# A kernel of recurrence and feed-forward network with its order written out: another list of steps and of PSUM tiles, the same operations

## The chip, the cores and the metric

One core of one Trainium2 chip runs the whole program. The metric is the device time of one execution in microseconds.

## The reference

Two blocks, one behind the other. The first is a recurrence over 768 tokens for 4 sequences of 8 heads, with a state of 40 by 40 per head:

```python
for t in range(S):
    y[:, :, t] = einsum('bhd,bhde->bhe', r_t, state)
    Sa = einsum('bhde,bhe->bhd', state, a_t)
    state = state * w_t[:, :, None, :] - einsum('bhd,bhe->bhde', Sa, b_t)
    state = state + einsum('bhd,bhe->bhde', v_t, k_t)
```

Its output, turned to 3072 tokens of 320 numbers, goes through an RMS norm with a gain and a gated feed-forward network with 1536 inner channels:

```python
xn = x / sqrt(mean(x * x) + 1e-6) * rms_g
g = xn @ w_gate
out = (g * sigmoid(g) * (xn @ w_val)) @ w_out
```

The three weight matrices arrive as 64-bit numbers and are narrowed to 32 bits on the chip; all else is 32 bits wide.

## The kernel before, in words

The work is cut into parts, each a function that notes steps. A step is one instruction on VectorE (DVE), ScalarE (ACT) or GpSimd (POOL), one DMA issue on SP, POOL or ACT, or one group of matmuls on TensorE (PE).

- `narrow` (12 slices of the weights, two parts each): load a part of the 64-bit weights, take the words apart on ScalarE and VectorE, and write the 32-bit slice to `sW` in DRAM.
- `front(c)` for each of 24 chunks of 32 tokens: load the tokens, turn them on TensorE, and build by doubling (levels of 2, 4, 8, 16 tokens, the group `gramk`) the decayed keys `KN` and the triangular matrix `LT`, which `where` steps copy from PSUM.
- `inverse(c)` (`early_inverse(c)` for the first four chunks): invert the triangular matrix by short VectorE steps (`tmp`, `Yi` or `M`), with `LT` and the inverse carried through DRAM (`sB`, `sY`).
- `main(c)`: the chunk itself: `state`, `lower`, `update`, `score`, the five `level` products, `y0`, and at the end the norm and the turned activations `xg`.
- `feed(g)` for each pair of chunks: 12 slices of the feed-forward network, two at a time: `h64` (8 passes through TensorE) and `h` (8 passes) for gate and value, SiLU on ScalarE (`sg`), the product on VectorE (`hT`), `out` (4 passes) summed up in `po`. After the first two groups six slices are kept in the buffers `wf` and the others come again from `sW`.

All 5924 steps, with what each needs, are noted first; nothing is issued then. `Plan.issue` goes through the text `ORDER` from front to back and issues one step a word; a `-` issues a pair of idle matmuls. Each word counts from the first step that has not been issued yet:

```python
i = first + int(word)
gone.add(i)
while first in gone:
    first += 1
```

So `ORDER` fixes the order on each engine and on each DMA queue, and engines run their queues strictly in order. What waits for what on the chip follows from the data alone.

A part of the steps works in PSUM. There are three pairs of banks (`ps0` to `ps2`) besides `po`, and 499 uses of a pair ("rooms"), from the first matmul that writes to the last reader. The text `PAIRS` has one digit a room that says which pair it takes; a room's first matmul waits until the room before it in the same pair has been read. The helpers record each operation at one line: L485 VectorE, L508 ScalarE copies, L511 ScalarE scalings, L524 DMAs, L527 matmuls, L530 turns.

Of the kernel before, what the change touches and what calls it, by code (L numbers as in the profile page):

```python
# [58 lines left out]
525 0 0 673 547 535 676 0 539 6 541 545 - 15 542 813 531 812 532 16 0 500 822 16 542 543 820 664 6 546 819 8 7 547  # L59
749 810 672 548 684 706 681 549 682 750 550 666 501 638 504 551 752 9 502 552 - 809 0 655 543 495 544 0 544 13 668  # L60
810 545 22 676 662 6 546 30 7 547 21 665 - 674 549 8 550 548 0 666 657 672 483 544 663 1139 660 32 658 671 23 675
807 5 0 662 0 802 801 538 662 804 667 803 673 805 817 666 15 809 7 808 672 539 8 17 822 1054 724 663 671 1064 670
834 846 600 1 479 540 806 480 541 9 481 10 0 0 673 804 8 539 15 672 9 671 813 666 812 540 541 479 852 674 0 15 722
806 541 17 22 807 725 0 667 714 807 717 722 799 715 483 - 800 808 484 805 806 818 820 819 724 814 801 725 829 810
# [4 lines left out]
737 738 1028 742 740 739 743 744 745 0 0 744 745 8 531 690 533 532 534 842 535 694 1042 14 695 - 1024 832 837 838  # L69
839 836 1045 1044 1043 1059 1047 1034 1064 1035 1046 536 1051 1052 1063 1074 1027 696 697 1037 1062 15 16 537 17  # L70
1036 1050 18 19 1075 1048 1073 913 1049 - 914 916 840 841 1058 843 917 919 921 918 920 844 538 539 845 846 540 542
# [6 lines left out]
622 396 705 480 624 699 706 703 942 702 700 337 338 339 340 543 541 701 - 548 341 342 343 344 704 345 346 349 348  # L78
347 - 350 549 397 941 546 398 708 952 - 709 720 354 715 698 634 635 714 399 400 716 721 733 729 718 353 717 636 719
# [1012 lines left out]
```

## Time and profile before

| | |
|---|---|
| median of 3 runs | 1012.74 us (1011.0 to 1017.76) |
| profiled execution | 1018.17 us |
| its span, from the first to the last instruction | 1016.1 us |
| mean granted TensorE clock | 0.972 |
| busy: TensorE, VectorE, ScalarE, GpSimd | 934.5, 794.0, 507.6, 310.7 us |
| moved by DMA | 112.97 MB |

Busy times are unions of an engine's instructions; PEld is the loading of weights into TensorE, which overlaps its matmuls. A wait is put down to what released it; "issue" stands for a wait that nothing in the program is seen to end. Times in a timeline row are the start from the span's beginning and the length, in us; a number in brackets is the engine's idle time just before, with its releaser.

### The profile page before, as it was taken

What the parts mean: (1) busy time and instruction counts of PE and PEld (TensorE: products, weight loads), DVE (VectorE), ACT (ScalarE), POOL (GpSimd) and SP (SyncE); (2) the same over time, 40 slices, a digit from 0 to 9 for tenths busy, and PEclk for the clock granted to TensorE, in tenths of its full rate; (3) what the DMA queues carried; (4) which work ended last, traced back from release to release, by engine and by line L of the source; (5) the groups of instructions that cost most, each with busy time, mean ns of one, the idle gap of its engine ahead of it and who ended that gap; (6) DMA issues with size and microseconds to landing.
All of it is one profiled execution on the core that took longest, in us unless ns stands there. A gap on an engine that the chain in (4) does not pass through costs nothing.

```text
span 1016.1 us, 55137 instructions
## 1 busy us (share of the span) xinstructions
PE 934.5 (92%) x24360; PEld 761.6 (75%) x24360; DVE 794.0 (78%) x2699; ACT 507.6 (50%) x1163; POOL 310.7 (31%) x554
## 2 busy tenths in 40 slices
PE   2647789799999999999999999999999999999998
PEld 2546677678787787888887888777878888778776
DVE  7798877778888988887988787877888897886310
ACT  5767784545446445544544454455454455443311
POOL 8635232241431342340350350331431431210000
PEclk9998679989999999999999999999999999999999
DMA  9975575744543635443544433624625533523122
GB/s 182 213 176 135 149 187 123 197 91 106 131 83 88 147 73 122 107 80 79 143 90 104 109 76 77 153 47 108 143 57 129 122 64 95 125 52 96 45 72 72
DMA packets 163534, 112.97 MB, mean 111 GB/s; under 512 B 124512, under 2 KB 142880, under 8 KB 163296
## 3 DMA queue, kind: packets, MB, share of 16 engines
q1 hardware_dynamic: 144928, 86.48, 34.3%
q0 software_dynamic: 16192, 22.64, 13.1%
q8 instruction: 191, 3.13, 1.3%
q10 hardware_dynamic: 2176, 0.33, 0.3%
q14 instruction: 47, 0.39, 0.1%
HBM read 93.39 MB, written 15.99 MB: 108 GB/s over the span
## 4 chain that ended last, share of the span: by engine, by line
PE 73%; DVE 13%; DMA 7%; issue 4%; ACT 1%; SPq 1%; POOL 1%; DVEq 0%; ACTq 0%; POOLq 0%
PE ps L527 52%; PE po L527 14%; PE ps L530 6%; DVE tmp L485 2%; DVE LT L485 2%; DVE Yi L485 2%; SPq L524 1%; DMA wf<-in_moe_w_gate_dram 1%; DVE K L485 1%; DMA wf<-sW 1%; DVE y L485 1%; DVE wf L485 1%; DVE As L485 1%; DMA wf<-in_moe_w_out_dram 1%; DMA rn<-in_r_dram 1%
## 5 line engine op out<-in xcount | busy, mean ns | idle before, releaser
L527 PE MATMUL ps<-xg,wf 128*128 128x256 f32 (+1 forms) x1728 | 356.5, 396 | 1.5 <-issue 1.2
L527 PEld LDWEIGHTS ps<-xg,wf 128*128 128x128 f32 (+1 forms) x1728 | 265.0, 192 | 50.1 <-issue 12.4
L527 PE MATMUL po<-wf,hT 128*128 128x320 f32 x576 | 178.9, 445 | 0.0
L485 DVE TENSOR_TENSOR tmp<-Yi,M 128x60 f32<-128x60 f32 (+24 forms) x620 | 130.3, 210 | 16.3 <-DMA M<-sB 1.7
L485 DVE TENSOR_TENSOR Yi<-Yi,tmp 128x60 f32<-128x60 f32 (+24 forms) x620 | 130.1, 210 | 15.5
L527 PEld LDWEIGHTS po<-wf,hT 128*128 128x128 f32 x576 | 103.2, 189 | 35.4 <-issue 0.7
L505 ACT ACTIVATE sg<-ps 128x512 f32<-128x512 f32 x72 | 43.0, 597 | 154.3 <-PE ps L527 142.6
L524 POOL DMA_DIRECT2D VU<-in_v_dram x92 | 53.7, 586 | 175.7 <-PE ps L527 127.9
L485 DVE TENSOR_TENSOR hT<-ps,sg 128x512 f32<-128x512 f32 x72 | 49.5, 687 | 69.5 <-ACT sg L505 69.2
L485 DVE TENSOR_TENSOR K<-K,T 128x512 f32<-128x512 f32 (+1 forms) x192 | 93.4, 496 | 9.7 <-PE ps L530 3.9
L527 PE MATMUL ps<-Ab,K 40*60 40x56 f32 (+2 forms) x4608 | 83.5, 228 | 15.5 <-DVE K L485 4.3
L527 PEld LDWEIGHTS ps<-Ab,K 40*60 40x60 f32 (+2 forms) x4608 | 74.6, 138 | 30.7 <-issue 13.6
L524 POOL DMA_DIRECT2D kbn<-in_k_dram x92 | 53.4, 583 | 135.7 <-PE ps L527 126.2
L508 ACT COPY KN<-ps 128x640 f32<-128x640 f32 x96 | 65.8, 693 | 43.6 <-PE ps L527 19.3
L508 ACT COPY K<-K 128x256 f32<-128x256 f32 (+1 forms) x168 | 72.3, 444 | 24.0 <-DVE K L485 8.8
L527 PEld LDWEIGHTS ps<-As,KN 128*40 128x40 f32 x3072 | 68.0, 127 | 18.3 <-issue 10.5
L485 DVE TENSOR_TENSOR As<-ps,msi 128x256 f32<-128x256 f32 (+1 forms) x168 | 69.8, 454 | 15.1 <-ACT As L511 8.6
L527 PE MATMUL ps<-As,KN 128*40 128x32 f32 x3072 | 73.8, 208 | 8.3 <-issue 6.0
L524 POOL DMA_DIRECT2D kbn<-in_b_dram x92 | 53.8, 587 | 88.0 <-PE ps L527 84.4
L524 POOL DMA_DIRECT2D wn<-in_w_dram x92 | 51.8, 567 | 68.6 <-DVE KN L485 32.3
L485 DVE TENSOR_TENSOR y<-y,ps 128x256 f32<-128x256 f32 x119 | 49.9, 419 | 18.8 <-PE ps L527 15.2
L485 DVE COPY_PREDICATED LT<-near,ps 128x384 f32<-128x384 uint32 (+2 forms) x72 | 52.3, 727 | 6.3 <-PE ps L527 5.4
(134 smaller groups left out, 1427.5 us busy)
## 6 DMA issues: line engine op xcount, KB each, us to landing
wf<-sW SPq DMA_DIRECT2D x82, 480.0 KB, 4.7
M<-sB SPq DMA_DIRECT2D x80, 128.0 KB, 2.9
rn<-in_r_dram SPq DMA_DIRECT2D x24, 160.0 KB, 5.2
out_dram<-o SPq DMA_DIRECT2D x48, 80.0 KB, 2.6
kbn<-in_b_dram POOLq DMA_DIRECT2D x92, 40.0 KB, 3.3
VU<-in_v_dram POOLq DMA_DIRECT2D x92, 40.0 KB, 2.7
kbn<-in_k_dram POOLq DMA_DIRECT2D x92, 40.0 KB, 3.2
wan<-in_w_dram POOLq DMA_DIRECT2D x46, 80.0 KB, 4.2
```

Of the source, the lines that this page charges most:

```text
L485: plan.add("DVE", kind, lambda at: fn(at(o), *m(at)), [o], aps(*args))
L505: plan.add("ACT", "act", lambda at: nc.scalar.activation(at(o), at(a), f, **kw), [o] + aps(acc), [a])
L508: plan.add("ACT", "copy", lambda at: nc.scalar.copy(at(o), at(a)), [o], [a])
L524: plan.add(by, "dma", lambda at: queue.dma_start(out=o, in_=i), [o], [i])
L527: return o, lhsT, rhs, lambda at: nc.tensor.matmul(at(o), lhsT, rhs, start=start, stop=stop, skip_group_check=True)
L530: return o, i, ident, lambda at: nc.tensor.transpose(at(o), i, ident)
```

## The change

Only the two texts differ. `ORDER` has the same 5944 words (5924 steps and 20 idle pairs) in another sequence, with its first 461 words and its last two steps as they were. `PAIRS` has the same 499 digits' places, of which 292 hold another digit. No function, operation, tile or number of buffers is changed. According to its description the order was searched by small moves, with every block of an engine's instructions taken to arrive later than was measured.

The diff is some 190 lines of numbers on either side; its beginning and its other part:

```diff
 156 157 654 663 681 665 519 684 678 679 682 877 664 675 163 166 167 164 868 29 171 680 165 168 677 434 435 30 523
-524 525 436 437 568 571 572 569 181 190 46 48 570 158 685 526 527 528 529 170 581 582 676 149 573 179 28 585 180
-574 182 870 191 169 686 690 530 531 532 533 534 535 536 537 538 539 687 172 683 540 541 199 542 694 200 202 543 544
...
+524 525 436 437 568 38 46 28 180 878 158 870 190 48 181 191 170 202 526 527 201 528 529 530 686 531 169 532 533 182
+534 535 570 536 537 149 572 538 200 539 569 540 179 541 571 542 543 685 581 683 544 545 546 547 573 548 582 549 199
...
 PAIRS = """
-1020102202110121001212001202211200201011102220012212101222200002201012220212110102101210221011100120120101220001012100
+1020102202110121111222000022000201112210001210020212001022110011120001020221210212021002122211202201212001112120210
...
```

More of the change, by code (lines that the diff above doesn't have):

```diff
@@ L48 @@
 156 157 654 663 681 665 519 684 678 679 682 877 664 675 163 166 167 164 868 29 171 680 165 168 677 434 435 30 523
[10 rows of a table removed]
[L59 to L62, printed above, removed]
@@ L63 @@
-834 846 600 1 479 540 806 480 541 9 481 10 0 0 673 804 8 539 15 672 9 671 813 666 812 540 541 479 852 674 0 15 722
-806 541 17 22 807 725 0 667 714 807 717 722 799 715 483 - 800 808 484 805 806 818 820 819 724 814 801 725 829 810
[4 rows of a table removed]
-737 738 1028 742 740 739 743 744 745 0 0 744 745 8 531 690 533 532 534 842 535 694 1042 14 695 - 1024 832 837 838
-839 836 1045 1044 1043 1059 1047 1034 1064 1035 1046 536 1051 1052 1063 1074 1027 696 697 1037 1062 15 16 537 17
-1036 1050 18 19 1075 1048 1073 913 1049 - 914 916 840 841 1058 843 917 919 921 918 920 844 538 539 845 846 540 542
[6 rows of a table removed]
@@ L78 @@
-622 396 705 480 624 699 706 703 942 702 700 337 338 339 340 543 541 701 - 548 341 342 343 344 704 345 346 349 348
-347 - 350 549 397 941 546 398 708 952 - 709 720 354 715 698 634 635 714 399 400 716 721 733 729 718 353 717 636 719
[35 rows of a table removed]
-763 765 774 764 592 773 766 388 593 771 594 654 595 389 772 596 434 597 655 598 599 600 646 601 602 658 - 603 712
[24 rows of a table removed]
-364 365 561 366 558 367 423 7 574 569 8 368 0 368 369 370 371 569 411 372 567 577 570 373 374 580 375 405 - 376 578
[3 rows of a table removed]
-- 422 423 643 424 0 726 424 0 424 567 570 739 967 372 751 571 977 572 425 573 959 640 574 426 575 428 576 978 427
@@ L145 @@
-577 723 578 642 579 968 652 580 724 429 581 970 582 375 583 0 583 372 584 727 585 732 373 586 587 652 762 1126 737
-430 731 3 653 735 375 654 743 1127 734 429 - 728 1 588 589 729 730 431 739 742 749 432 435 746 741 590 591 745 592
-744 642 593 594 595 437 596 645 597 644 598 747 599 756 600 755 646 748 436 771 754 759 757 760 761 601 602 643 740
-751 438 439 767 603 604 605 752 763 655 766 433 - 656 764 606 753 775 607 608 389 773 765 609 610 659 772 390 611
[5 rows of a table removed]
-357 546 591 358 328 359 360 361 540 404 544 536 405 557 406 408 407 0 - 544 536 542 537 538 550 0 409 552 0 545 550
[10 rows of a table removed]
@@ L165 @@
-747 758 755 756 757 623 624 761 625 626 627 628 629 760 630 740 751 444 754 741 631 440 - 445 753 446 752 763 659
[23 rows of a table removed]
-362 363 192 364 402 365 366 563 367 564 368 558 413 - 369 404 370 371 574 372 415 373 573 5 555 374 406 572 408 389
[5 rows of a table removed]
-41 202 49 203 738 356 50 341 40 204 205 350 42 358 43 253 206 353 44 165 256 207 254 366 208 368 209 45 - 359 360
[9 rows of a table removed]
-- 556 364 225 365 366 412 565 226 367 368 411 409 575 414 407 573 406 0 575 416 403 368 573 369 370 371 412 372 373
[27 rows of a table removed]
[10 rows of a table added]
+673 547 535 676 0 539 6 541 545 - 15 542 813 531 812 532 16 0 500 822 16 542 543 820 6 546 664 819 8 7 547 810 672
@@ new lines @@
+548 749 684 706 681 549 682 550 666 501 638 504 551 665 502 809 9 750 0 495 542 - 742 543 544 0 544 13 668 22 810
+545 676 662 6 30 546 7 21 674 8 547 0 656 - 540 483 541 539 32 666 657 672 23 544 663 1139 660 658 0 666 670 802 0
+662 0 802 801 804 803 805 538 662 666 7 667 673 817 15 809 8 808 672 663 539 17 822 1054 724 671 1064 670 834 846
+600 1 479 540 806 480 541 9 481 10 0 0 673 804 8 539 672 15 9 671 813 666 812 540 541 479 852 674 0 15 722 806 541
+17 22 807 725 676 0 807 714 717 722 799 715 483 - 800 808 484 805 806 818 820 819 724 814 801 725 829 668 817 669
[4 rows of a table added]
@@ new lines @@
+742 740 739 743 744 745 0 0 744 745 8 531 690 533 532 534 842 535 694 1042 14 695 - 1024 832 837 838 839 836 1045
+1044 1043 1059 1047 1034 1064 1035 1046 536 1051 1052 1063 1074 1027 696 697 1037 1062 15 16 537 17 1036 1050 18 19
+1075 1048 1073 913 1049 - 914 916 840 841 1058 843 917 919 921 918 920 844 538 539 845 846 540 542 1076 847 1072
[6 rows of a table added]
+480 624 699 706 703 942 702 700 337 338 339 340 543 541 701 - 548 341 342 343 344 704 345 346 349 348 347 - 350 549
+397 941 546 398 708 952 - 709 720 354 715 698 634 635 714 399 400 716 721 733 729 718 353 717 636 719 730 637 351
[36 rows of a table added]
@@ new lines @@
+606 607 608 434 710 609 610 554 701 611 612 613 711 646 435 774 662 666 1 777 663 756 775 432 436 776 437 668 - 448
[23 rows of a table added]
+558 566 365 366 367 423 7 574 569 8 368 0 368 369 370 371 569 411 372 567 577 570 373 374 580 375 405 - 376 578 413
+377 579 419 507 0 398 404 500 416 409 716 406 0 406 411 574 412 407 575 409 573 226 416 421 572 227 369 370 229 417
+422 228 418 414 554 720 566 721 719 509 709 419 420 423 726 371 424 722 372 425 712 373 374 375 426 376 377 427 727
+970 731 3 - 730 4 710 378 651 728 381 979 729 562 5 379 508 565 711 380 428 736 579 0 574 0 574 725 0 568 574 575
@@ new lines @@
+421 576 569 0 576 421 373 422 577 423 0 577 578 970 579 423 580 581 424 639 582 725 425 583 640 374 967 427 584 428
+585 375 977 426 586 723 734 642 587 968 652 739 724 727 429 959 588 1127 589 738 0 977 727 - 746 732 589 1 590 750
+731 653 375 372 728 429 654 762 3 771 652 748 734 1127 735 744 743 430 736 729 747 749 591 745 592 730 742 739 431
+432 435 741 556 755 756 760 754 759 642 593 594 437 595 646 596 761 597 598 645 599 757 600 740 643 601 436 602 644
+751 438 439 767 752 763 603 655 604 605 766 433 - 656 606 764 753 607 775 608 389 609 765 773 610 647 611 774 390
[5 rows of a table added]
@@ new lines @@
+357 358 359 535 545 404 540 536 543 406 546 405 547 544 408 0 - 556 406 536 537 538 0 409 358 359 315 557 546 0 409
[11 rows of a table added]
+389 668 775 441 390 773 772 660 765 632 667 670 666 768 451 - 673 662 672 665 767 778 556 770 762 453 771 661 769
[22 rows of a table added]
+389 402 192 364 365 564 366 413 - 367 404 572 368 563 369 554 575 403 370 5 371 415 574 372 555 373 573 558 374 406
[11 rows of a table added]
+351 531 352 189 538 532 0 - 527 539 726 345 544 736 556 346 12 528 229 727 11 531 201 529 347 728 4 348 349 532 725
+202 542 324 735 350 555 401 351 543 352 6 353 405 354 537 403 402 552 355 404 356 0 356 537 398 324 357 358 552 532
@@ L233 @@
+359 540 539 360 4 549 533 534 547 535 544 553 6 548 563 7 407 561 565 361 550 362 0 - 558 355 400 552 356 551 537
[29 rows of a table added]
 """
 PAIRS = """
-1020102202110121001212002211200201011102220012212101222200002201012220212110102101210221011100120120101220001012100
-0102202021021021110211202211221001122102012222002200002010212222110112021012020112110021010021101100100210001102220
-2222120001100121202121222012220211100100221101011011202011210112221221112100100100010202210011011021222022221002020
-0020100220112100111020021122212220211212110101012000002221112010012120201112122211102102111002010100000201101010101
@@ L240 @@
-211221011020020202020112210001002212121
+1020102202110121111222000022000201112210001210020212001022110011120001020221210212021002122211202201212001112120210
+1210010102122101101202210022001110112012012222002111101011220200012021000110201210120121120022121122100211001120000
+0221210021120222202021202102221111100211220010102000221101211112002120112000100122100212211000101120212022221000120
+0121100220021221011010211022202211011211112102022101002220220120012100201221201110102101022101010000201022022002022
@@ L241 @@
+212102210212010210010220102112111210210
 """
```

314 rows, old and new, of the table ORDER are left out of this document.

## The prediction

> **What bounds the kernel now.** I read the page first, then the table of stages, TensorE's waits in the long stage, and the timeline around single waits.
>
> ```profile
> span 1016.1 us, 55137 instructions
> PE 934.5 (92%) x24360; PEld 761.6 (75%) x24360; DVE 794.0 (78%) x2699; ACT 507.6 (50%) x1163; POOL 310.7 (31%) x554
> q8 instruction: 191, 3.13, 1.3%
> 0.00:110.00 110.00, 61.35 (x2016) 54.86 (x2016) 91.84 (x264) 74.97 (x153) 62.18 (x132) 0.92 0.87 179
> 110.00:250.00 140.00, 125.38 (x3472) 102.12 (x3471) 109.13 (x348) 80.63 (x184) 37.08 (x64) 0.89 0.56 134
> 250.00:1010.00 760.00, 746.11 (x18830) 603.58 (x18819) 593.04 (x2090) 351.34 (x825) 211.43 (x358) 1.00 0.43 98
> ```
>
> The last three rows are stages: length, busy time of PE, PEld, DVE, ACT and POOL, granted clock, DMA share, GB/s. From 250 us on TensorE is busy for 746.11 of 760 us. Idle there is 13.9 us, and since the operations stay the same, that idle time and whatever the clock loses is all that a new order can win in this stage. The first 110 us are not TensorE's: it idles 48.65 us, while VectorE is busy for 91.84.
>
> What TensorE waits for from 250 us on:
>
> ```profile
> PE ps L527 <- issue: 10.3, 14, 1.8
> PE ps L530 <- issue: 1.5, 1, 1.5
> PE ps L527 <- ACT x L511: 0.4, 1, 0.4
> PE ps L527 <- DVE K L485: 0.4, 1, 0.4
> PE ps L530 <- DVE LT L485: 0.3, 1, 0.3
> PE ps L527 <- DVE LT L485: 0.3, 1, 0.3
> ```
>
> Fifteen waits, 11.8 us, have no releaser in the program ("issue"); the other engines cost only 1.4 us. The instruction queue explains the fifteen: 3.13 MB in 191 packets is 16.4 KB each, and 2 x 24360 instructions over 191 packets are 255 a packet, so TensorE's program arrives in blocks of some 127 passes. One of the waits:
>
> ```profile
> 555.19 0.80 PE L527 MATMUL ps<-As,KN 128*40 128x32 f32 x32
> 555.82 0.79 PE L527 MATMUL ps<-As,kbn 128*40 128x32 f32 x32
> 556.44 1.39 PE L527 MATMUL ps<-As,KN 128*40 128x32 f32 x63
> 559.65 0.84 PE L527 MATMUL ps<-As,KN 128*40 128x32 f32 x33 [1.82 <-issue]
> 560.80:564.20 3.40, 3.40 (x10) 2.68 (x9) 2.57 (x11) 0.00 (x0) 2.40 (x5) 0.50 0.97 230
> ```
>
> 127 small passes, a whole block, go through in 2.64 us (555.19 to 557.83); then TensorE stands for 1.82 us in the middle of a group of like matmuls. So a block that consists of small passes is consumed faster than the next one comes. The last row shows the aftermath: 3.4 us at half clock, 1.7 us more.
>
> [...]
>
> How long a block lasts depends on what is in it (rows from 250 us on):
>
> ```profile
> L527 PE MATMUL ps<-xg,wf 128*128 128x256 f32 x1024 | 246.4, 391 | 1.2 <-issue 1.2
> L527 PE MATMUL po<-wf,hT 128*128 128x320 f32 x520 | 160.9, 445 | 0.0
> L527 PE MATMUL ps<-xg,wf 64*128 64x256 f32 x512 | 70.3, 396 | 0.0
> L527 PE MATMUL ps<-As,KN 128*40 128x32 f32 x2560 | 57.1, 203 | 3.3 <-issue 3.1
> ```
>
> Busy time over count: 0.24, 0.31 and 0.14 us a pass in the feed-forward part, 0.022 in the recurrence. A feed step (h of 8 passes, out of 4, h64 of 8) is therefore 1.9, 1.2 or 1.1 us of cover for the next block; a recurrence step of 32 to 64 passes is 0.7 to 1.4 us.
>
> **The change, counted.** I decoded both lists of steps and compared them engine by engine. The fewest steps that must be lifted out to turn one queue into the other are 81 of 905 on TensorE, 580 of 2696 on VectorE, 322 of 1144 on ScalarE, 127 of 545 on GpSimd's queue and 129 of 634 on SP's. By their place in the profile: none before 65 us; 1, 20, 16, 8 and 16 from 65 to 110 us; one (VectorE) from 110 to 250; all others later. TensorE's steps move at most four places. 292 of the 499 tile uses in PSUM get another of the three bank pairs. Nothing is added or removed, so the busy times stay and the sum has three terms.
>
> **Term 1, the start (65 to 110 us).**
>
> ```profile
> 80.80 0.68 DVE L485 TENSOR_SCALAR wf<-wf 128x480 int32<-128x480 int32 x1 [0.90 <-ACT o L505]
> 81.25 0.29 PE L527 MATMUL ps<-rE,vut 40*64 40x32 f32 x1
> 82.06 0.17 DVE L485 TENSOR_TENSOR M<-M,tmp 64x15 f32<-64x15 f32 x1
> 82.57 0.63 ACT L511 ACTIVATE M<-M 32x256 f32<-32x256 f32 x1
> 83.66 1.43 SPq L524 DMA_DIRECT2D sB<-LT  x3
> 85.13 0.45 SPq L524 DMA_DIRECT2D sY<-M  x1
> 96.63 0.73 PE L527 MATMUL ps<-M,LT 16*16 16x16 f32 x64 [1.08 <-ACT Sd L508]
> 99.97 0.84 PE L527 MATMUL ps<-M 16*32 16x16 f32 x48 [1.11 <-issue]
> ```
>
> The inverse of chunk 1 moves ahead: its last VectorE step (82.06) no longer stands behind the weight step that waits 0.90 us, its scaling (82.57) passes two weight activations, its second write to sY (85.13) passes three writes of sB, 1.43 us. But the matmul that uses it (96.63) waits for a ScalarE copy that frees its bank pair, and the next one (99.97) for its block. The copy moves up by three short copies. I take -0.5; at best both waits go, -2.2. Against it, VectorE's next step now is a scaling of scores, whose last matmul ends at 81.54 us, so the weight steps behind it on VectorE slip, and with them the SP write of sW and the loads of the inverse that queue behind that write: at worst +2.0, about the 0.90 us wait twice.
>
> **Term 2, the late blocks (250 us on).** In the 6 us ahead of the fifteen waits the change moves a feed step at only four, each among its neighbours. At the wait shown, an out step of 1.2 us moves from behind a recurrence step to ahead of it, which shortens the cover behind it rather than lengthening it. [...] I take -1.0. The bounds: all fifteen go, with two halvings of the clock, -11.8 - 3.4 = -15.2; or the two shortened blocks stand 1.8 us each, +3.6.
>
> [...]
>
> **Term 3, new waits for PSUM.** TensorE takes a bank pair as soon as its last reader is done:
>
> ```profile
> 535.25 1.49 DVE L485 COPY_PREDICATED LT<-near,ps 128x256 f32<-128x256 uint32 x2
> 536.80 1.14 PE L527 MATMUL ps<-xg,wf 64*128 64x256 f32 x8
> 537.51 0.27 DVE L485 TENSOR_TENSOR Ab<-Ab,T 128x128 f32<-128x128 f32 x1
> 537.71 0.20 DVE L485 TENSOR_TENSOR tmp<-Yi,M 128x60 f32<-128x60 f32 x1
> 537.94 0.22 DVE L485 TENSOR_TENSOR Yi<-Yi,tmp 128x60 f32<-128x60 f32 x1
> ```
>
> The reader ends at 536.74, the h64 matmuls start at 536.80. In the new list six VectorE steps that came after this reader stand ahead of it (the last three rows and three like them, some 1.2 us as they overlap), while TensorE's queue ahead is the same 1.9 + 1.9 + 1.0 us: the pair comes free 1.1 us late, unless VectorE started earlier. I did this for all 387 refills from 250 us on (work moved ahead of the reader against work moved ahead of the matmul, both by the profile's durations). Before, 62 have under 0.2 us to spare; after it, 40 come out late, by 12.6 us together, against 5 and 1.2 before. So +11.4 if nothing gives way, and 0 if VectorE's idle time (760 - 593 = 167 us in this stage) takes all of it. The nearest row is the 1.4 us that TensorE waits for the other engines now, so I take a value near the low end, a quarter, +3.0.
>
> **The sum.** The profiled execution took 1018.17 us, 2.1 more than its span; -0.5 - 1.0 + 3.0 makes 1019.7 in such an execution. The three timed runs have a median of 1012.74, 5.4 lower, and the same terms make 1014.2. A change of under 1% (10.1 us) is about what a measurement of this kernel cannot tell from none: my forecast is no change.
>
> **The rivals.** *Faster*: the order does cover the late blocks. For it: fifteen waits at one cause, each only 0.3 to 1.8 us short. Against it: the cover ahead of eleven of them is not touched. With all gone, 1012.74 - 0.5 - 15.2 = 997.0; it decides from two thirds of them, 10.1 of 15.2. *Slower*: PSUM pairs come free late because VectorE's and ScalarE's steps were spread for a TensorE that stands at its block edges, and it does not stand there. Its place is the refills of term 3 from 280 to 940 us; the price +11.4, and 1.7 for the half clock at each of the two refills that come out more than 1 us late, +3.4: 1027.5. It decides from 10.1 us, when nearly nothing is absorbed. For it: the 62 refills without slack and 292 pairs dealt anew; against it: 167 us of idle VectorE. *It does not do what it says*: lateness comes from what else the DMA engines carry when a block is fetched (DMA share 0.97 in the 3.4 us after the wait shown), which the order does not govern. Then term 2 is 0 and the time 1015.2, within the forecast. *The start slips*: +2.0 in place of -0.5, 1016.7, also within it.
>
> **How the numbers follow.** No change 0.46 (the last two rivals included), faster 0.22, slower 0.32; slower is likelier than faster because term 3 touches 40 places and term 2 four. The likeliest case alone reaches from 1004 to 1022. The range for eight in ten takes in most of both other cases, 999 to 1030.
>
> **What would show it.** Right: PE busy near 934, issue waits from 250 us on again 8 to 14 us in a dozen or more places, waits of TensorE for DVE and ACT there 2 to 6 us instead of 1.4, the first feed-forward matmul within 1 us of before. Term 2 is wrong if issue waits fall under 4 us; term 3 if waits for DVE and ACT exceed 9 us or stay at 1.4; term 1 if 110 us is reached more than 2 us earlier or later. The forecast is wrong below 1002.6 or above 1022.9.

## The result and the profile after

The changed kernel takes 1019.59 us (median of 19 runs, 1015.15 to 1024.05); the kernel before takes 1012.43 in 19 runs beside them. The ratio is 1.0072, 95% interval 1.0052 to 1.0091: slower by some 7 us, under the 1% that I called no change.

The two profiled executions hide this: 1017.78 us after, 1018.17 before. The page, the stages and TensorE's waits of the changed kernel (columns as in the prediction):

```profile
span 1016.0 us, 55133 instructions
PE 938.6 (92%) x24360; PEld 762.6 (75%) x24360; DVE 794.4 (78%) x2699; ACT 508.6 (50%) x1163; POOL 311.7 (31%) x554
q8 instruction: 191, 3.13, 1.3%
0.00:110.00 110.00, 63.30 (x2044) 56.56 (x2044) 92.29 (x270) 75.69 (x156) 64.13 (x132) 1.00 0.86 181
110.00:250.00 140.00, 128.65 (x3614) 104.84 (x3611) 111.39 (x353) 80.81 (x183) 38.68 (x68) 0.94 0.56 140
250.00:1010.00 760.00, 745.33 (x18650) 600.42 (x18649) 590.74 (x2078) 351.45 (x823) 208.84 (x355) 0.99 0.41 96
```

```profile
PE ps L527 <- issue: 10.2, 15, 2.1
PE ps L530 <- issue: 1.3, 1, 1.3
PE ps L527 <- DVE As L485: 0.9, 3, 0.3
PE ps L527 <- DVE Yi L485: 0.4, 1, 0.4
PE ps L527 <- ACT x L511: 0.4, 1, 0.4
PE ps L530 <- ACT vut L508: 0.3, 1, 0.3
PE ps L530 <- ACT x L511: 0.3, 1, 0.3
PE ps L527 <- DVE tmp L485: 0.3, 1, 0.3
PE ps L527 <- DVE LT L485: 0.2, 1, 0.2
```

A block here is a piece of 256 instructions of TensorE's program (the trace has 24360 matmuls, as many weight loads and 290 others, 256.6 for each of the 191 packets; the late blocks stand at one place of 256, see below), an edge is where one block ends and the next begins, and a late block is a wait at an edge that no other engine ends ("issue" in the rows). Operations, instruction blocks and the total of late blocks from 250 us on (11.5 us against 11.8) are as before, and waits for other engines there are 2.8 us against 1.4. In both traces the operations of VectorE (2699), ScalarE (1137) and GpSimd (554) and the DMA issues of SP (634) start in the order in which the program lists them. The granted clock in the first two stages is 1.00 and 0.94 against 0.92 and 0.89: this execution happened to lose little to half clock in its start (this profiled run's mean clock is 0.986, the median of the 19 runs 0.970). The first 1400 steps take 226.1 us against 230.0 and the others 785.2 against 781.6, so the start covers here what the change costs later. So I did not compare two whole profiles, but the same stretches of the list in many: the time from the end of the last matmul before one list position to that before another, at positions where both orders have issued the same steps.

One stretch stood out, list steps 4650 to 5140 (about 750 to 826 us): 74.7 us before, 81.4 after. TensorE's timeline there, the old order first:

```profile
758.17 2.42 PE L527 MATMUL po<-wf,hT 128*128 128x320 f32 x8
760.52 0.78 PE L527 MATMUL ps<-ST,aP 40*32 40x40 f32 x64
761.23 0.40 PE L530 MATMUL ps<-ident,x 64*128 64x64 f32 x6
761.46 0.61 PE L530 MATMUL ps<-ident,kbn 64*104 64x64 f32 x16
762.00 0.79 PE L527 MATMUL ps<-VU,LT 32*32 32x40 f32 x64
```

Then the new order:

```profile
752.09 2.42 PE L527 MATMUL po<-wf,hT 128*128 128x320 f32 x8
754.79 0.94 PE L530 MATMUL ps<-ident,kbn 64*104 64x64 f32 x16 [0.27 <-ACT x L511]
755.54 0.37 PE L530 MATMUL ps<-ident,x 64*128 64x64 f32 x6
755.84 0.78 PE L527 MATMUL ps<-ST,aP 40*32 40x40 f32 x64
756.55 0.61 PE L527 MATMUL ps<-VU,LT 32*32 32x40 f32 x42
759.29 0.62 PE L527 MATMUL ps<-VU,LT 32*32 32x40 f32 x22 [2.12 <-issue]
```

Both have the same two output steps (x8) and behind them the same matmuls: 64 for the state of chunk 18 (`ST,aP`), 6 and 16 turns, then `lower` (`VU,LT`). In the old order the state stands first, in the new one the 16 turns of `fr20.26` do (step 26 of `front(20)`; `ma` and `fe` stand for `main` and `feed`). 64 + 6 + 16 + 42 = 128 matmuls with their weight loads are 256 instructions, one block: an edge lies right behind the output steps and the next one 42 matmuls into `lower`, where the new order stands for 2.12 us. Within this wait, some 1.5 us after TensorE stopped at 757.16, the clock halves; window 758.68 to 768.88 us of the new order:

```profile
758.68:768.88 10.20, 9.59 (x124) 7.67 (x124) 7.73 (x28) 2.29 (x5) 2.00 (x4) 0.50 0.59 102
```

2.1 us of standing and half of 10.2 us make 7.2; the stretch is 6.7 longer. The instruction queue shows when the block was fetched. Its row in the window of the old order's two output steps, 758.17 to 760.59 us:

```profile
q8 instruction: 1, 0.02, 3.9%
```

In the new order no packet of this queue starts in the windows 752.09 to 754.51 (the output steps) and 754.51 to 756.40; it starts at 756.43, seen in the window 756.40 to 757.90:

```profile
q8 instruction: 1, 0.02, 5.8%
```

So the old order has the block fetched while long passes run. The new one has it fetched only behind the edge: the small passes behind the output steps end at 757.16 us, 0.7 us after the packet's start.

### The profile page after: what moved, and what is told of

It is laid out like the page before. It is cut to its first block, busy times and chain, and to the rows that moved or that the text cites. A ratio compares the mean times of both kernels' runs of the same rounds, so it can differ in the third digit from the quotient of the medians.

```text
span 1016.0 us, 55133 instructions
## 1 busy us (share of the span) xinstructions
PE 938.6 (92%) x24360; PEld 762.6 (75%) x24360; DVE 794.4 (78%) x2699; ACT 508.6 (50%) x1163; POOL 311.7 (31%) x554
## 4 chain that ended last, share of the span: by engine, by line
PE 76%; DVE 10%; DMA 5%; issue 4%; ACT 2%; POOL 1%; SPq 1%; DVEq 0%; ACTq 0%; POOLq 0%
PE ps L527 54%; PE po L527 14%; PE ps L530 7%; DVE tmp L485 2%; DMA wf<-in_moe_w_gate_dram 1%; DVE LT L485 1%; DVE Yi L485 1%; DVE As L485 1%; DVE K L485 1%; POOL kbn L524 1%; PE po L1059 1%; DVE wf L485 1%; DMA wf<-in_moe_w_out_dram 1%; DMA rn<-in_r_dram 1%; SPq L524 1%
## 5 line engine op out<-in xcount | busy, mean ns | idle before, releaser
L485 DVE TENSOR_TENSOR tmp<-Yi,M 128x60 f32<-128x60 f32 (+24 forms) x620 | 131.4, 212 | 16.4 <-DMA M<-sB 0.8
L527 PE MATMUL ps<-Ab,K 40*60 40x56 f32 (+2 forms) x4608 | 82.9, 228 | 11.4 <-DVE K L485 4.0
L527 PE MATMUL ps<-As,KN 128*40 128x32 f32 x3072 | 74.8, 208 | 7.2 <-issue 4.1
L485 DVE TENSOR_TENSOR y<-y,ps 128x256 f32<-128x256 f32 x119 | 49.9, 419 | 18.1 <-PE ps L527 15.2
```

The source lines that it names most:

```text
L485: plan.add("DVE", kind, lambda at: fn(at(o), *m(at)), [o], aps(*args))
L527: return o, lhsT, rhs, lambda at: nc.tensor.matmul(at(o), lhsT, rhs, start=start, stop=stop, skip_group_check=True)
```

## The experiments

Kernels of one group ran on one chip, 6 or 12 runs each, beside 29 runs of the kernel before. Their lists are the old and the new one joined at positions where both have issued the same steps, with the PSUM pairs renamed to fit. The first kernel of the first group is the kernel before itself.

**before_again**: no edit.

> The kernel before, unchanged, once more: it gives the granted clock of each execution and a second profile. All theories: ratio 1.000 within 0.3%. If block edges set the time, the clock varies between executions and the slower executions are those with the lower clock.

1018.33 us, ratio 0.9987 (0.9956 to 1.0018). Two samples of one kernel differ by about 0.1%, and on this chip it takes some 6 us more than in the first comparison.

**start_new** and **rest_new**:

```diff
 ORDER  start_new: steps 1 to 1400 (to about 230 us)   -old +new
 ORDER  rest_new:  steps 1401 to the end               -old +new
```

> New order and pairs up to about 230 us (step 1400 of the list), the order before from there on. PSUM theory (the loss is new waits of TensorE for VectorE and ScalarE after 250 us): within 0.2% of before. Start theory (the reordered 65 to 110 us are slower, or send later loads into a worse place): slower by the whole 0.7%, 7 us.

> The order before up to about 230 us, the new order and pairs from there on. PSUM theory: slower by 0.5 to 0.8% (5 to 8 us), with TensorE's waits for VectorE and ScalarE after 250 us at 3 us or more against 1.4 before. Start theory: within 0.2% of before.

start_new 1.0030 (0.9994 to 1.0066), rest_new 1.0034 (0.9994 to 1.0075). Neither theory came out as stated: each half carries about half of the cost, and neither interval alone shuts out zero. But the stretch of steps 4650 to 5140 takes 74.7 us in before_again and start_new, which have the old order there, and 79.7 in rest_new, again with a late block at the same place.

**after_half_block**: the new order with half a block of instructions more at the front, which moves all edges by 64 passes. The added matmuls write to a part of a bank that nothing reads.

```diff
     with tc.manual_schedule():
+        for _ in range(32):
+            nc.tensor.matmul(po_[0:32, 0, DM:DM + 32], ident[0:32, 0:32], ident[0:32, 0:32],
+                             start=False, stop=False, skip_group_check=True)
         plan.issue(ORDER, PAIRS)
```

> The changed kernel with 32 small matmuls (64 passes, 128 instructions of TensorE) ahead of all steps, in the first 10 us where TensorE waits for loads: every edge of an instruction block falls half a block earlier among the steps. PSUM theory: as the changed kernel, 1.005 to 1.009 of before. Block theory (the loss is where the edges fall): it moves, by 3 us or more, either way; 0.998 to 1.004 if the new order was unlucky in its edges.

1075.4 us, ratio 1.0566 (1.0504 to 1.0628). TensorE's waits for blocks from 150 us on:

```profile
PE ps L527 <- issue: 38.3, 30, 3.7
PE ps L530 <- issue: 4.2, 3, 2.4
PE po L527 <- issue: 1.3, 1, 1.3
```

43.8 us, against 15.2 in the changed kernel from there on, and 76 us at half clock against 31: 28.6 of standing and 22.7 of halved clock, out of the 55.9 us by which this span (1071.9) is longer. So how good this list is depends on where the edges fall. The old list was not tried with moved edges.

**mid_new** and **mid_old** exchange 471 steps, of which 435 stand elsewhere:

```diff
 ORDER  mid_new: old list, steps 4664 to 5134   -old +new
 ORDER  mid_old: new list, steps 4664 to 5134   -new +old
```

> The old order with only list steps 4663 to 5134 (about 752 to 825 us, 435 places differ) in the new order. Theory of one place: the stage of steps 4650 to 5140 takes 79 to 82 us instead of the 74.7 us of the old order, with a late instruction block of about 2 us in the matmuls of lower for chunk 18 (L527) and 7 to 10 us at half clock behind it; the whole time is 4 to 6 us above before, ratio 1.004 to 1.006. Rival, spread costs: the new order loses a little in every stage, and this stage of a thirteenth of the list carries about 0.5 us: ratio 1.000 to 1.001 and the stage within 1.5 us of 74.7. Rival, chance: the late block of this stage falls here in one execution and elsewhere in another; the stage differs from 74.7 us by what other stages do from run to run (1 to 2 us), ratio 0.998 to 1.002.

> The new order with only list steps 4663 to 5134 put back to the old order. Theory of one place: the stage of steps 4650 to 5140 is back at 74 to 76 us without a late block in it; the whole is 1 to 3 us above before, ratio 1.001 to 1.003, against the 1.0072 of the whole change. Rival, spread costs: ratio 1.006 to 1.007, as all other stages keep the new order. Rival, chance: ratio 1.005 to 1.009, and the stage within 2 us of 81.

mid_new 1.0104 (1.0050 to 1.0159), its stretch 81.4 us with the late block (1.8 us) and 10.2 us at half clock. mid_old 1.0017 (0.9986 to 1.0047), its stretch 74.9 without either. Spread costs and chance are out for this stretch: it follows the order of these steps alone. mid_new lost 10 us in its six timed runs; the interval's low end is the 5 us expected, and the place alone explains no more. In its profile late blocks after step 1400 take 19.2 us in all, and 22.8 us there are at half clock, against 11.8 and 10.4 in the kernel before. Of this, 3.8 us is one block near 576 us whose wait changes from execution to execution (see Term 2 below).

**swap_in** and **swap_out** move two steps each (steps between them that keep their order are left out):

```diff
 swap_in (old list)            swap_out (new list)
   ma16.56 scale (ScalarE)       fr20.21 copy (ScalarE)
   ma17.46 scale (ScalarE)     + fr20.25 copy (ScalarE)
 + fr20.24 copy (ScalarE)        ma17.46 scale (ScalarE)
 + fr20.26 turn (TensorE)        ma16.56 scale (ScalarE)
   ma18.0 state (TensorE)      + ma18.0 state (TensorE)
 - fr20.24 copy                  fr20.26 turn (TensorE)
   ma17.48 turn3 (TensorE)     - fr20.25 copy
 - fr20.26 turn                  ma17.48 turn3 (TensorE)
                               - ma18.0 state
```

> The old order with two steps moved: the copy that frees the third PSUM pair and the transposes of fr20.26 (turn) stand ahead of the state matmuls of chunk 18 instead of behind them, as in the new order. TensorE's queue now meets a wait of about 0.3 to 0.5 us on ScalarE right after the output passes of the feed-forward, where the old order let it run ahead over a block edge. Theory of one place: the next block is asked for 1 us or more later than before (after the edge, not 1.4 us ahead of it), a matmul behind it starts about 2 us late and 3 to 10 us at half clock follow; stage 4650 to 5140 takes 78 to 81 us, ratio 1.003 to 1.006. Rival, the wait alone: the step costs its own 0.3 to 0.5 us, stage 75.0 to 75.5 us, ratio 1.000 to 1.001.

> The new order with two steps moved: a ScalarE copy of fr20.25 stands ahead of the scale of ma17.46, which frees a PSUM pair some 0.7 us earlier, and the state matmuls of chunk 18 stand ahead of the transposes of fr20.26, as in the old order. Theory of one place: TensorE's queue runs ahead over the edge during the output passes, the late block of 2 us behind it goes away and with it the half clock; stage 4650 to 5140 takes 74.5 to 76.5 us instead of 81.4, ratio to before 1.001 to 1.003. Rival, the 435 other places of this stage are what costs: the stage stays at 79 to 82 us, ratio 1.005 to 1.008.

swap_in 1.0051 (1.0015 to 1.0086), stretch 79.0 us:

```profile
766.77 1.03 PE L530 MATMUL ps<-ident,kbn 64*104 64x64 f32 x16
767.73 0.78 PE L527 MATMUL ps<-ST,aP 40*32 40x40 f32 x64
768.44 0.40 PE L530 MATMUL ps<-ident,x 64*128 64x64 f32 x6
768.77 0.61 PE L527 MATMUL ps<-VU,LT 32*32 32x40 f32 x42
771.36 0.41 PE L527 MATMUL ps<-VU,LT 32*32 32x40 f32 x22 [1.98 <-issue]
```

swap_out 1.0042 (1.0008 to 1.0075), stretch 74.9 us; `lower` runs through:

```profile
773.01 0.78 PE L527 MATMUL ps<-ST,aP 40*32 40x40 f32 x64
773.72 0.73 PE L530 MATMUL ps<-ident,kbn 64*104 64x64 f32 x16
774.27 0.37 PE L530 MATMUL ps<-ident,x 64*128 64x64 f32 x6
774.57 0.79 PE L527 MATMUL ps<-VU,LT 32*32 32x40 f32 x64
```

Two steps of 5924 make the late block and take it away. swap_out's time is above the 1.001 to 1.003 that I expected, though its interval takes these in; what the start costs is still in it.

**pair_free** and **swap_in_free** keep TensorE's order of after and of swap_in, and give the turns a PSUM pair that is free earlier:

```diff
 pair_free (new list)                        swap_in_free (old list)
 + ma16.56 scale ahead of ma17.46 scale      + fr20.26 turn, then fr20.24 copy,
                                               ahead of ma18.0 state
 PAIRS from fr20.26 turn on: 1 <-> 2         PAIRS from fr20.26 turn on: 0 <-> 1
```

> The new order with TensorE's order left as it is, but without the wait of 0.27 us ahead of the transposes of fr20.26: one ScalarE step (a scale of ma16.56) stands ahead of the scale of ma17.46, and the second and third PSUM pairs change places from there on, so that the transposes go to a pair which is free before the output passes end. Theory that the wait holds TensorE's queue ahead of the block edge: the block is asked for about 1 us before the edge, no late block follows, stage 4650 to 5140 takes 74.5 to 76 us, ratio 1.001 to 1.004. Rival, that it is the kind of matmuls on both sides of the edge (16 transposes, then 64 small matmuls, in this order) and not the wait: the block is asked for 1 us or more behind the edge again, the stage takes 79 to 82 us, ratio 1.005 to 1.008.

> The old order with the transposes of fr20.26 ahead of the state matmuls of chunk 18, as in the run that moved them there and lost 4.3 us in this stage, but with the first and second PSUM pairs exchanged from there on, so that the transposes find a free pair and the state matmuls take the one that comes free later. Theory that the wait is the cause: the transposes start without a stop, the stage takes 74.5 to 76 us, ratio 0.999 to 1.002. Rival, the kind of matmuls on both sides of the edge: 78 to 81 us, ratio 1.003 to 1.006. A mixed result is possible, since the state matmuls now wait on ScalarE in the middle of the block behind the edge.

pair_free 1.0089 (1.0062 to 1.0117), swap_in_free 1.0043 (1.0012 to 1.0075); stretches 78.2 and 81.5 us, each with the late block. The timeline of pair_free:

```profile
765.19 0.77 PE L530 MATMUL ps<-ident,kbn 64*104 64x64 f32 x16
765.78 0.38 PE L530 MATMUL ps<-ident,x 64*128 64x64 f32 x6
766.08 0.78 PE L527 MATMUL ps<-ST,aP 40*32 40x40 f32 x64
766.79 0.61 PE L527 MATMUL ps<-VU,LT 32*32 32x40 f32 x42
769.52 0.41 PE L527 MATMUL ps<-VU,LT 32*32 32x40 f32 x22 [2.12 <-issue]
```

The 0.27 us wait is gone and the 2.12 us are not. My theory that the array's visible wait makes the block late falls; the rival, which of the two groups stands first at the edge, holds.

**late_new_mid_old** and **after_again**:

```diff
 ORDER  late_new_mid_old: steps 1401 to 4663 and 5135 to the end   -old +new
 ORDER  after_again: the new list
```

> The old order up to list step 1400 (about 230 us) and in steps 4663 to 5134, the new order in the rest. Theory of one place: with the start and this place old, nothing of the change's cost is left, ratio 0.998 to 1.001, stages from 1400 on together 784 to 787 us as in before. Rival, the rest of the new order loses too: ratio 1.002 to 1.004. If the start carries the 1.0017 to 1.0042 that the two kernels with the place put back still lost, this kernel is 2 us or more faster than they are.

> The new order unchanged, on the chip of the kernels beside it. All theories: ratio 1.005 to 1.009, as in the first comparison (1.0072), and stage 4650 to 5140 again 79 to 82 us; if the late block of that stage were chance, the stage would be within 1.5 us of 74.7 in this profile with about even odds.

late_new_mid_old 1.0002 (0.9975 to 1.0029), after_again 1.0089 (1.0056 to 1.0122). With the start and the one place old, no cost is seen any more, within some 3 us; nor is there a gain, so no version here beats the kernel before.

All profiled executions at the one place (stretch of steps 4650 to 5140; packet is the start of the block's packet less the end of the output steps; all in us):

```
                    first at edge  stretch  late block  half clock  packet   ratio of times
before              state          74.7     0           0           -1.36
before_again        state          74.7     0           0           -1.41    0.9987
start_new           state          74.7     0           0           -0.93    1.0030
mid_old             state          74.9     0           0           -0.88    1.0017
swap_out            state          74.9     0           0           -0.94    1.0042
late_new_mid_old    state          75.1     0           0           -1.00    1.0002
after               turn           81.4     2.1        10.2         +1.91    1.0072
after_again         turn           78.4     1.8         3.4         +2.29    1.0089
rest_new            turn           79.7     1.8         6.8         +2.26    1.0034
mid_new             turn           81.4     1.8        10.2         +2.14    1.0104
pair_free           turn           78.2     2.1         3.4         +1.65    1.0089
swap_in             turn           79.0     2.0         3.4         +2.15    1.0051
swap_in_free        turn           81.5     2.1        10.2         +1.45    1.0043
```

Seven against six, without overlap: 79.9 us on average against 74.8, +5.1.

**Why the turns hold the fetch back** no kernel of its own tests; the traces' records speak for one reason. Beside the matmuls and weight loads TensorE's program has 287 separate semaphore instructions, and the trace has a record of each, put down to TensorE's sequencer and not to the array. Four of them stand around these turns (three in swap_in_free) and none around the state. In the order after they run at 753.24, 754.78, 755.10 and 755.22 us, the first two ahead of the edge and the others 14 and 17 instructions behind it. The first has all 8 matmuls of the output steps ahead of it in the program and runs before the last four of them, which start at 753.28 to 754.08 us: here the sequencer is ahead of the array. In pair_free one runs at 765.02, right behind the ScalarE scale that ends at 764.97 and frees a pair. So this instruction came only with the scale, like the one at 754.78 in the order after, 0.04 us behind the scale that ends at 754.74; but here the array ran through.

The program gives the place of the edges, counted in instructions (two a pass, and one for each of the sequencer's own): all 185 waits over 0.25 us without a releaser after step 1400, in the 13 executions, stand at one place of the 256 or one instruction beside it. Around this place 1087 separate semaphore instructions stand, from 40 ahead of it to 31 behind it, and for 1070 of them the packet starts at least 0.9 us later than they run. From 32 to 71 behind it, that holds for only 262 of 538. My estimate from these counts alone is that the block is asked for when the sequencer is some 32 instructions past the place where the array would stand. This fits swap_in_free: of its three such instructions the one ahead of the edge runs 3.8 us before the packet, but the two that stand 12 and 15 behind the edge run 1.7 and 1.6 us before it. Of 496 weight loads from 40 ahead to 31 behind that wait over 0.2 us for another engine by themselves, 351 have the packet start sooner than 0.9 us after them.

So a packet that starts sooner than 0.9 us is rare behind such a semaphore instruction (17 of 1087) and common behind a weight load that waits (351 of 496). Why the two differ was not shown; that the turns' semaphore instructions hold the request back here, and the state's matmuls do not, is my reading of the counts. It is not the only reason for a late block: 85 of the 185 follow one of the 411 edges that have such an instruction from 40 ahead to 31 behind, 100 follow one of the 1565 that have none.

## Why the prediction was right or wrong, step by step

**The forecast** of no change held, on the slow side: +0.72% against +0.15%, 1019.6 us against 1014.2. That it held owes something to luck: the sum was 5 us short, by two terms and partly against a gain that I did not see, and the band of 1% had room for that. The sign that I named for term 2, issue waits of 8 to 14 us, came true with other blocks than I counted. The *Slower* rival did not come about by its mechanism (refills of PSUM at 40 places), and *Faster* came true for about a third of the late blocks' time.

**Term 1 (start, -0.5; bounds -2.2 and +2.0) had the wrong sign.** The first large group of matmuls behind the moved steps, before and then after:

```profile
111.03 1.93 PE L527 MATMUL ps<-rE,vut 40*64 40x32 f32 x64 [0.90 <-DVE M L485]
109.32 1.93 PE L527 MATMUL ps<-rE,vut 40*64 40x32 f32 x64 [2.62 <-DVE M L485]
```

In these two executions the new order is 1.7 us earlier. Over all of them it starts at 107.4 to 111.0 us in seven with the old start (mean 109.1) and 109.3 to 113.1 in six with the new one (mean 111.2), with a wait on VectorE of up to 0.9 us in the former and 1.5 to 2.7 in the latter. So +2.1, the worst bound: the wait is on VectorE, as that bound said (which of its steps slip is not shown), and I chose the other end. By 170 us the means differ by 3.4 us, but single executions spread over 9, so the rest of this stays open. The times agree: with the new start and the old place 1.0030, 1.0017 and 1.0042.

**Term 2 (late blocks, -1.0; bounds -15.2 and +3.6) was wrong at one block and better than I thought elsewhere.** Issue waits of 0.25 us or more at blocks from 340 us on, in six executions with the old order there and seven with the new one:

```
block (time before)   old order                       new order
 64 (354 us)          0.8 0.8 1.0 1.0 0.9 1.7         0   0   0   0   0   0   0
104 (546)             1.2 0.7 0.7 1.2 1.0 0.7         0   0   0   0   0   0   0
107 (560)             1.8 0.5 0   0   1.8 0           0   0   0   0   0   0   0
170 (868)             0.8 0.5 0.5 0.5 0.8 0.8         0   0   0   0   0   0   0
113 (589)             0   0   0   0   0   0           1.6 1.3 1.6 1.3 1.3 1.6 1.6
171 (875)             0   0   0   0   0   0           0   0.9 0.9 1.2 0   1.1 2.0
110 (576)             0   0.9 4.3 3.8 0   2.1         0   1.7 0   0   0   0   0
all but 148, mean     11.3                            7.4
```

Late blocks at the first six of these places belong to the order, though how long they are, and for blocks 107 and 171 whether they come, changes; block 110 comes and goes within one order. The new order took 3.9 us of late blocks away on average (7.8 to 12.9 us in an execution with the old order, 5.0 to 8.9 with the new one), some 1.6 of them at block 110. Among the blocks that went is the one that the prediction showed (block 107), where I had found that the move shortens the cover. Block 148 alone gave back 5.1.

The step that failed is the count of cover behind the -1.0 and the two shortened blocks of the +3.6: it took each block to be asked for 36 passes ahead of an edge, an estimate of mine that no run shows, and passes by their durations alone. By that count the blocks at risk were those near 524 and 775 us; no execution of either order stands there, and the one near 760 us was not on the list because its passes are the same in both. What differs is when the packet starts, and no fixed distance describes it: behind the same output steps the packet starts 1.4 us before their end or up to 2.3 us after it. The upper bound also had no half clock in it, which is more than half of the 5.1.

**Term 3 (refills, +3.0) was right in kind.** Waits for DVE and ACT from 250 us on are 2.8 us, within the 2 to 6 named. The gross +11.4 was absorbed nearly whole: the average over executions from step 1400 on is 1.7 us of such waits in the old order and 3.4 in the new one, so +1.7, half of the term. late_new_mid_old holds most of it, and no loss shows in its time.

**The sum as it came out**: +2.1 to 3.4 (start), +5.1 (block 148), -3.9 (other late blocks), +1.7 (refills): +5.0 to +6.3 us, against 7.3 measured (ratio 1.0072; its interval is 5.3 to 9.2). The parts come from single profiled executions, and the half clock behind the other late blocks is not in them. By them late_new_mid_old would be 2.2 us faster than before; its interval, 2.5 us faster to 2.9 slower, neither shows nor excludes that. The first feed-forward matmul starts at 130.0 us against 131.4, outside the 1 us that I named.

*It does not do what it says* is out: the order does decide which blocks are late. That the search does not know what makes a packet late is my reading, not tested.

## What to carry to other kernels

In this kernel TensorE's program came in by blocks of 256 instructions, and how good the new order is depended on where their edges fell: with half a block more at the front it took 57 us longer than the kernel before. Look at what stands on both sides of each edge, and put long passes ahead of it. The packet started in time where the state stood behind the long passes (0.9 to 1.4 us before their end, six executions), and 1.5 to 2.3 us after it where the turns with their semaphore instructions stood there (seven); by the counts, such instructions up to some 30 behind the edge matter. A stretch of small matmuls as long as a block ran through in 2.4 us (754.79 to 757.16 in the order after), and TensorE went on 2.9 us after the packet's start (756.43 to 759.29), so its successor has to be asked for before it begins. Price a late block with its half clock (3.4 to 10.2 us of it here), and don't compare two whole profiles where the start alone (the first 1400 steps) takes from 225.7 to 242.5 us: compare the same stretch of the list in several executions.

## What the runs showed of the hardware

- A late block of 1.8 to 2.1 us was followed by 3.4, 6.8 or 10.2 us at half clock, in steps of 3.4 (the seven executions of the table). In the order after it began some 1.5 us into the wait of 2.12 us.
- A packet of the instruction queue takes 0.9 to 2.4 us here (median 1.1, 13 executions), and where TensorE stands over 1 us for a block from block 64 (354 us) on, it goes on 1.2 to 1.6 us after the packet's end (45 waits).
- 64 idle passes at the front put the new order 57 us above the kernel before (after_half_block, ratio 1.0566); in the profile 51 of the 56 us more than in the changed kernel are late blocks and half clock.
